# An add of tap products in a convolution and state-space kernel: by VectorE, or by an accumulating transfer inside SBUF issued by GpSimd

## The chip, the cores and the metric

The kernel runs on one core of a Trainium2 chip. The metric is the device time of one execution in microseconds (us), as the median of its runs; lower is better. A profile is one execution, recorded by the hardware profiler, with its own span. Engines are named as in the profile: PE (TensorE's matmuls; PEld its weight loads), DVE (VectorE), ACT (ScalarE), POOL (GpSimd) and SP (SyncE, which issues loads).

## The reference

Two independent layers over a sequence of S = 2048 with D = 1024 channels, all in bf16; their outputs stand side by side in the last dimension.

```
# A: gated convolution
k_shift[s] = sum over t of k[s - 3 + t] * shift_k[:, 3 - t]     # 4 taps, per channel
kv = k_shift * v
y  = irfft(rfft(kv, 2S) * rfft(ssm_k, 2S))[:S]  + kv * ssm_D    # long causal convolution
a  = q * y
# B: diagonal complex state space model
h[t] = Lam_bar * h[t-1] + x[t] @ B_bar^T
b = 2 * Re(h @ C^T) + x * Dskip
out = concat([a, b], -1)
```

The change is in the first line of A: the sum of the four tap products.

## The kernel before

**Tiling of A.** A row s of the sequence is written s = 16 n1 + n2, with n1 (128 values) on the partitions and n2 = 0 to 15 as the number of a tile. For each n2, four steps make one tile of kv, [128 x 1024] bf16:

- kvm(n2), lines 547 to 555: multiplies four neighbouring rows of k (from a ring of eight, `kring`) by the four taps (`wbc`): a tile `m` of [128 x 4 x 1024], some 2.3 us on DVE, in one instruction or, where the ring wraps, in two (L553, L555).
- kva(n2), line 560: adds the upper two products to the lower two, in place: `m[:, 0:2] += m[:, 2:4]`, 2048 elements on each partition. This is the changed line.
- kvb(n2), line 566: adds the last two into `st["kv", n2]` (named acc in the profile).
- kvc(n2), line 568: multiplies by v.

Then PE transforms the tile along n1 (am(n2, w), L573, four matmuls), ACT copies the results out of PSUM (ae, L580), and GpSimd stores them to HBM (ast, L582, tensor `Ys_kv`). The filter ssm_k takes the same way: hT and hc transpose it, hd adds ssm_D into one row (L605, on DVE), hm multiplies by the same matrix (L612), he copies out (L618), hst stores (two transfers each, L625, tensor `Ys_h`). When all 16 tiles of both are in HBM, the second stage loads them back in another layout (lk and lh, L635), transforms along n2 (sk, sh: L642), multiplies (pr, L667), transforms back (sa, L676), and a third stage (a3, L702) ends with q (qm, L712) and the output.

**Layer B** goes on beside it in 16 chunks of 128 rows: U (L462, matmuls with B), ue (ACT), r1 and r2 (rotation, DVE: L474, L483), rc, sc (scan, L493), cm, ca, r3, r4 (DVE), y (L517, matmuls with C), ye, yst. B's tile for the rotation products has the same name and slots as kvm's `m`.

**Order.** Nothing is scheduled by a tool: a hand-written list, ORDER (from line 66), names the tasks one after another, such as `kvm.4:m1 kva.4 kvb.4:b6`. Each engine takes its part of the list in order. `kva.4` is kva with n2 = 4; what follows the colon are the slots of the ring buffers that a task takes: `m0` and `m1` (two slots for products), `b0` to `b14` (2 KB per partition: kv, ysb, ysbh and others), `a..` (larger), `p0` to `p7` (PSUM banks). A task that takes a slot waits until the last user of the slot is done, the store of an output slot among them. The framework sets all semaphores from the tiles that an instruction reads and writes. The tap tasks run in the order n2 = 1, 3, 2, 0, 4, 6, 5, 7, 8, 10, 9, 13, 11, 12, 15, 14 (kvm), all in the first 180 us; kva in the order 3, 1, 2, 0, 4, 6, 5, 7, 10, 9, 8, 11, 12, 15, 14, 13. Some stretches of the list, with other tasks left out:

```
kvm.1:m0 ... kvm.3:m1 ... kva.3 stt ... kvb.3 ... kva.1 ... kvm.2:m1 ... kva.2 kvb.1 kvc.1 kvm.0:m0 kvb.2 kvc.2 kva.0 kvb.0 kvc.0 kvc.3
he.1.1.3 hst.1.1.1 ... kvm.4:m1 kva.4 kvb.4:b6 ... yst.1 ... hst.0.1.0 kvm.6:m0 kva.6 he.1.3.2:b3 ... kvm.5:m1 ... kvb.6:b8
hst.2.0.0 kva.5 ue.5.2 kvc.6 kvb.5:b7 kvc.5 ... kvm.7:m0 ... hst.2.3.1 hm.2.2.0:p4 kva.7 kvb.7:b1 kvc.7
kvm.10:m1 kva.10 kvb.10:b11 ... kvm.9:m1 kva.9 kva.8 kvb.8:b5 kvb.9:b6 ... kvm.11:m0 kva.11 ... kvb.11:b3
kvm.12:m0 ... kva.12 ... kvb.12:b4 kvc.12 kvm.15:m0 kva.15 kvb.15:b0 ... kvm.14:m0 ... kva.14 kva.13 kvb.14:b1 kvc.14
```

**Queues.** SP issues all loads. GpSimd issues nearly all stores (`gpd`), one after another and in the order of the list; it does next to nothing else. An issue that waits holds up those behind it.

Of the kernel before, what the change touches and what calls it, by code (L numbers as in the profile page):

```python
# [14 lines left out]
ALU = mybir.AluOpType  # L15
# [161 lines left out]
def full_kernel(ctx, tc, A_q, A_k, A_v, A_shift_k, A_ssm_k, A_ssm_D, B_x, B_Lre, B_Lim, B_Bre, B_Bim,  # L177
# [3 lines left out]
    nc = tc.nc  # L181
# [375 lines left out]

    def kva(n2):
        m = st["km", n2]
        nc.vector.tensor_add(m[:, 0:2, :], m[:, 0:2, :], m[:, 2:4, :])  # L560
    E["kva"] = kva

    def kvb(n2):
# [217 lines left out]
```

## Time and profile before

| | |
|---|---|
| median of 2 runs | 395.23 us (393.83 to 396.62) |
| span of the profiled execution | 399.6 us, 4.4 above that median |
| PE / DVE / ACT / POOL busy | 361.3 / 331.0 / 281.3 / 92.9 us |
| L560 (kva) on DVE | 16 instructions, 1205 to 1227 ns each, first at 25.8, last at 175.1 us |
| L566 (kvb) on DVE | 16 instructions, 671 to 693 ns each |
| DMA | 101.38 MB, mean 254 GB/s |
| chain that ended last | PE 43%, DMA 21%, issue 13%, ACT 9%, POOL 6%, DVE 5% |

In the timelines a row has its start and its length in us, the engine, the line, the operation, what is written and read, the count (rows that follow one another are merged, "x2"), and in brackets the idle time ahead of it with what ended it. The slices of the page cut the span into 40 equal parts of 10 us; a digit is the busy share in tenths. The issue rows give a transfer, the queue, the number, the size of one and the median us from issue to landing. The wait rows give who waited for whom: total us, times, longest. The DVE rows of L560 and L566 belong to kva and kvb in the order given above, so the n-th row of L560 is the n-th kva of the list; in the same way the rows of L582 and L625 on POOL are ast and hst.

### The profile page before, as it was taken

Reading aid. Unit: us, or ns where it says so; the run is one execution under the profiler, and the core shown is the slowest. Engines: PE = TensorE matmul, PEld = TensorE weight load, DVE = VectorE, ACT = ScalarE, POOL = GpSimd, SP = SyncE. Lnnn points to the kernel's source line nnn. Section 1 sums busy time; section 2 is a strip of 40 time slices with the busy share of each in tenths; the row PEclk is TensorE's granted clock in tenths of the full one; section 3 lists DMA queues with packets and bytes.
Section 4 is the critical chain, followed back from the end, with each engine's and each line's share of the span. In section 5 each row is a group of like instructions: output and inputs, shape, how many; then the busy total and the mean of one; then the engine's idle time right before and its main releaser. Section 6 shows DMA issues by size and latency. Waiting matters only on the chain.

```text
span 399.6 us, 8799 instructions
## 1 busy us (share of the span) xinstructions
PE 361.3 (90%) x3486; PEld 245.6 (61%) x3529; DVE 331.0 (83%) x335; ACT 281.3 (70%) x519; POOL 92.9 (23%) x156
## 2 busy tenths in 40 slices
PE   4899997998999887998999998999889999999990
PEld 2799986665665755886755644555335577744440
DVE  4999999997789588689989986989949558999920
ACT  4998888857688854778598787778657785374440
POOL 2000022465655763433001010110011003001450
PEclk9999999999999996999999999999999999999997
DMA  6999996578976898697898969979596987899781
GB/s 240 286 294 275 281 194 229 164 246 301 286 218 226 197 242 219 167 347 229 237 232 265 328 194 287 268 238 310 170 300 198 300 201 310 300 388 347 264 308 60
DMA packets 61124, 101.38 MB, mean 254 GB/s; under 512 B 31102, under 2 KB 33150, under 8 KB 61084
## 3 DMA queue, kind: packets, MB, share of 16 engines
q1 hardware_dynamic: 50428, 67.13, 60.3%
q0 software_dynamic: 10656, 33.71, 23.6%
q8 instruction: 27, 0.44, 0.5%
q14 instruction: 13, 0.11, 0.1%
HBM read 52.57 MB, written 33.55 MB: 216 GB/s over the span
## 4 chain that ended last, share of the span: by engine, by line
PE 43%; DMA 21%; issue 13%; ACT 9%; POOL 6%; DVE 5%; SPq 1%; another core or an unknown queue 1%; POOLq 0%; ACTq 0%; DVEq 0%
PE ps_u L462 16%; PE ps_y L517 11%; DMA Ys_h<-ysbh 8%; PE ps_a L676 5%; DMA hab<-hab 4%; PE ps_a L642 4%; DMA Ys_kv<-ysb 4%; POOL Ys_h L625 3%; ACT ysbh L618 2%; ACT hab L650 2%; POOL Ys_kv L582 2%; DMA l2k<-Ys_kv 1%; DMA wts<-a_c_W 1%; PE ps_t L427 1%; ACT vsb L683 1%
## 5 line engine op out<-in xcount | busy, mean ns | idle before, releaser
L462 PEld LDWEIGHTS <-BT 128*128 128x128 bf16 x2048 | 121.4, 99 | 12.0 <-issue 1.7
L517 PE MATMUL ps_y<-CT,h 128*128 128x512 bf16 x491 | 126.8, 381 | 2.1 <-ACT ysbh L618 1.2
L462 PE MATMUL ps_u<-xT,BT 128*128 128x128 bf16 x2048 | 127.5, 220 | 0.5 <-DVE BT L438 0.3
L517 PEld LDWEIGHTS <-h 128*128 128x128 bf16 x512 | 45.9, 98 | 43.8 <-issue 0.6
L493 DVE TENSOR_TENSOR_SCAN h<-rtab,h 128x1024 bf16<-128x1024 f32 x32 | 71.9, 2280 | 0.4
L667 DVE TENSOR_TENSOR hab<-x,hab 128x2048 bf16<-128x2048 bf16 x32 | 38.3, 1222 | 21.8 <-DMA hab<-hab 17.4
L625 POOL DMA_DIRECT2D Ys_h<-ysbh x64 | 46.0, 721 | 31.2 <-ACT ysbh L618 29.6
L464 ACT CAST u<-ps_u 128x512 bf16<-128x512 f32 x64 | 38.0, 613 | 13.0 <-PE ps_u L462 12.4
L618 ACT CAST ysbh<-ps_a 128x512 bf16<-128x512 f32 x64 | 35.5, 604 | 14.6 <-DMA Ys_h<-ysbh 5.6
L650 ACT CAST hab<-ps_a 128x512 bf16<-128x512 f32 x64 | 35.9, 620 | 12.3 <-PE ps_a L642 10.5
L656 ACT CAST x<-ps_a 128x512 bf16<-128x512 f32 x64 | 36.5, 614 | 10.6 <-PE ps_a L642 9.8
L580 ACT CAST ysb<-ps_a 128x512 bf16<-128x512 f32 x64 | 35.5, 614 | 11.0 <-DMA Ys_h<-ysbh 3.8
L683 ACT CAST vsb<-ps_a 128x512 bf16<-128x512 f32 x64 | 36.0, 618 | 5.6 <-PE ps_a L676 5.6
L474 DVE TENSOR_TENSOR mt<-u,Z 128x4096 bf16<-128x4096 bf16 x16 | 36.5, 2284 | 2.1 <-ACT u L464 2.1
L582 POOL DMA_DIRECT2D Ys_kv<-ysb x32 | 17.6, 553 | 87.1 <-ACT ysb L580 87.0
L685 POOL DMA_DIRECT2D Vs<-vsb x16 | 8.5, 534 | 124.5 <-ACT vsb L683 111.1
L474 DVE TENSOR_TENSOR mt<-h,Z 128x4096 bf16<-128x4096 bf16 x16 | 36.6, 2287 | 0.2
L676 PE MATMUL ps_a<-hab,wts 128*128 128x512 bf16 x125 | 32.6, 379 | 2.5 <-DVE hab L667 2.2
L528 ACT CAST yo<-ps_y 128x512 bf16<-128x512 f32 x32 | 19.0, 605 | 21.0 <-PE ps_y L517 16.6
L553 DVE TENSOR_TENSOR mt<-kring,wbc 128x4096 bf16<-128x4096 bf16 (+3 forms) x16 | 30.0, 1883 | 0.1
L612 PE MATMUL ps_a<-hT,F1t 128*128 128x256 bf16 x128 | 21.8, 276 | 7.8 <-ACT ysb L580 2.7
L522 PE MATMUL ps_y<-Dd,xT 128*128 128x128 bf16 x128 | 28.0, 219 | 0.3
(108 smaller groups left out, 417.4 us busy)
## 6 DMA issues: line engine op xcount, KB each, us to landing
Ys_kv<-ysb POOLq DMA_DIRECT2D x32, 256.0 KB, 3.5
Ys_h<-ysbh POOLq DMA_DIRECT2D x64, 128.0 KB, 3.7
l2h<-Ys_h SPq DMA_DIRECT2D x16, 512.0 KB, 5.2
hab<-hab SPq DMA_DIRECT2D x64, 128.0 KB, 5.6
l2k<-Ys_kv SPq DMA_DIRECT2D x16, 512.0 KB, 5.2
Vs<-vsb POOLq DMA_DIRECT2D x16, 512.0 KB, 5.8
vv<-Vs SPq DMA_DIRECT2D x32, 256.0 KB, 5.5
kring<-in_A_k_dram SPq DMA_DIRECT2D x8, 512.0 KB, 4.7
```

Of the source, the lines that this page charges most:

```text
L462: nc.tensor.matmul(pu[:, w, jl, :], BT[:, 2 * jp + jl, w, d, :], xT[:, d, :], start=(d == 0), stop=(d == ND - 1))
L464: E["ue"] = lambda i, jp: nc.scalar.copy(st["u", i][:, :, 2 * jp:2 * jp + 2, :], st["pu", i, jp][:])
L474: nc.vector.tensor_mul(m, s_, win(Z))
L493: nc.vector.tensor_tensor_scan(gf, rt1, gf, 0.0, ALU.mult, ALU.add)
L517: nc.tensor.matmul(py[:], h[:, 1 - w, j, :], CT[:, j, w, dh * 512:(dh + 1) * 512], start=(j == 0 and w == 0), stop=(j == NJ - 1 and w == 1))
L618: nc.scalar.copy(st["yh", qd, n4, w // 2][:, :, w % 2, :], st["pa", qd, n4, w][:].rearrange("p (c d) -> p c d", c=2))
L625: gpd(Ys_h[cc, n0:n0 + 2, :, qd * DQ:(qd + 1) * DQ].rearrange("n k d -> k n d"), t_[:, cc, :, :])
L650: nc.scalar.copy(st["hab", g][:, 0, cols], pt[:])
L656: nc.scalar.copy(st["x16", g][:, w * 512:(w + 1) * 512], st["ps", "l2k", g, w][:])
L667: nc.vector.tensor_mul(hab[:], st["x16", g][:].unsqueeze(1).to_broadcast([P, 2, D]), hab[:])
L676: nc.tensor.matmul(pt[:], st["w", gq][:, gi, 1 + a, :], hab[:, a, w * 512:(w + 1) * 512], start=(a == 0), stop=(a == 1))
L683: nc.scalar.copy(st["vsb", gq][:, gi, w * 512:(w + 1) * 512], st["ps", "v", g, w][:])
```

## The change

kva(n2) is no longer an instruction of DVE. GpSimd issues a transfer that reads `m[:, 2:4, :]` in SBUF and adds it to `m[:, 0:2, :]` in SBUF: 128 partitions of 2048 elements, 512 KB. ORDER is not changed, so the issue stands on GpSimd's queue where kva stands in the list. The framework lets the issue wait for kvm(n2) and lets kvb(n2) wait for the end of the transfer.

```diff
     def kva(n2):
         m = st["km", n2]
-        nc.vector.tensor_add(m[:, 0:2, :], m[:, 0:2, :], m[:, 2:4, :])
+        nc.gpsimd.dma_start(m[:, 0:2, :], m[:, 2:4, :], accum_op=ALU.add)
     E["kva"] = kva
```

## The prediction

> **What bounds the kernel now.** I read the page first (busy shares, slices), then VectorE's (DVE's) and GpSimd's (POOL's) timelines for the stretch in which the changed line runs (20 to 180 us), then the DMA issues and the waits.
>
> ```profile
> PE 361.3 (90%) x3486; PEld 245.6 (61%) x3529; DVE 331.0 (83%) x335; ACT 281.3 (70%) x519; POOL 92.9 (23%) x156
> ...
> DVE  4999999997789588689989986989949558999920
> ...
> PEclk9999999999999996999999999999999999999997
> ```
>
> No engine is free: PE is busy 90% of the span, DVE 83%. Until 90 us DVE is full; from 90 to 180 it has small gaps, while PE's slices stay at 8 or 9. Every engine issues in the order of the hand-written list, so a late result of one stops the next in line on another. GpSimd, at 23%, looks idle, but it issues the stores, in order.
>
> ```profile
> 88.92 1.23 DVE L560 TENSOR_TENSOR mt<-mt 128x2048 bf16<-128x2048 bf16 x1
> 92.79 0.69 DVE L566 TENSOR_TENSOR acc<-mt 128x1024 bf16<-128x1024 bf16 x1 [2.64 <-DMA Ys_h<-ysbh]
> ...
> 143.78 2.36 DVE L560 TENSOR_TENSOR mt<-mt 128x2048 bf16<-128x2048 bf16 x2
> 146.23 1.29 DVE L566 TENSOR_TENSOR acc<-mt 128x1024 bf16<-128x1024 bf16 x2
> ...
> 160.56 1.22 DVE L560 TENSOR_TENSOR mt<-mt 128x2048 bf16<-128x2048 bf16 x1
> 165.14 0.69 DVE L566 TENSOR_TENSOR acc<-mt 128x1024 bf16<-128x1024 bf16 x1 [3.36 <-DMA Ys_h<-ysbh]
> ...
> 168.79 1.23 DVE L560 TENSOR_TENSOR mt<-mt 128x2048 bf16<-128x2048 bf16 x1
> 170.21 0.69 DVE L566 TENSOR_TENSOR acc<-mt 128x1024 bf16<-128x1024 bf16 x1 [0.19 <-ACT ysb L580]
> ```
>
> In these DVE lines the second add (kvb, L566) stands close behind the first (kva, L560): 0 to 4 us lie between. Whatever replaces L560 has to be done within that.
>
> ```profile
> 94.73 1.43 POOL L625 DMA_DIRECT2D Ys_h<-ysbh  x2 [1.89 <-ACT ysbh L618]
> ...
> 105.39 1.43 POOL L625 DMA_DIRECT2D Ys_h<-ysbh  x2
> 114.38 4.32 POOL L625 DMA_DIRECT2D Ys_h<-ysbh  x6 [7.57 <-ACT ysbh L618]
> ...
> 181.29 0.54 POOL L582 DMA_DIRECT2D Ys_kv<-ysb  x1 [2.04 <-ACT ysb L580]
> ```
>
> GpSimd's timeline: most issues wait for an ACT eviction (the bracket). An issue put behind one of them inherits that wait.
>
> ```profile
> Ys_kv<-ysb POOLq DMA_DIRECT2D x32, 256.0 KB, 3.5
> Ys_h<-ysbh POOLq DMA_DIRECT2D x64, 128.0 KB, 3.7
> ...
> Vs<-vsb POOLq DMA_DIRECT2D x16, 512.0 KB, 5.8
> ```
>
> The last number is the time from issue to landing in us: 5.8 for 512 KB from GpSimd's queue.
>
> ```profile
> ACT ysbh L618 <- DMA Ys_h<-ysbh: 5.6, 4, 2.9
> ...
> PE ps_a L573 <- DVE acc L568: 0.7, 1, 0.7
> ```
>
> Two links already bind somewhere: ACT waits for stores to free its output slots, and PE waits for the finished kv tile (L568). Delays on DVE and GpSimd therefore have a way back into ACT and PE.
>
> **The change, part by part.**
>
> *Removed:* 16 adds on DVE at 1.22 us (L560), 19.6 us of DVE time, all before 177 us.
>
> *Added:* 16 issues on GpSimd at 0.54 to 0.74 us (its DMA rows), about 9 us on a queue 23% busy; and 16 transfers of 512 KB which read their destination too.
>
> *The new wait.* kvb(n) must wait until the transfer has landed. I call "lag" the time from the start of the issue to that moment. The trace has no accumulating transfer. Lower end 3.5 us (Ys_kv row, 256 KB); upper end 10.4: two rows of this queue, 256 KB in 3.5 and 512 KB in 5.8, differ by 2.3 per 256 KB, and if the extra read of 512 KB costs as much again, that is 5.8 + 4.6. I take 5.8, the row of the same size and queue: both ends of this transfer lie in SBUF, which should pay part of the extra read. The Trainium skill (DMA: Bandwidth & Descriptors, Anatomy of one DMA) gives about 2.0 us plus bytes at 436 GB/s, and its page Collectives: The Full Stack (Why ReduceScatter is half of AllGather) says an adding transfer reads two sources; my estimate from both is 2.0 + 1.05 MB/436 GB/s = 4.4 us, and the sum below would then be +45 and the time 440. The Vs row, 5.8 for a plain 512 KB where that formula gives 3.2, speaks for the longer lag.
>
> *The new order.* In the changed program's order on GpSimd, kva.4 stands behind hst.1.1.1 (the pair of Ys_h stores at 94.73), kva.6 ahead of hst.1.2.0 (101.17), kva.5 behind hst.2.0.0 (ends 118.7), kva.7 behind hst.2.3.1 (ends 133.0), kva.11 behind hst.3.3.0 (ends 162.6), kva.14 behind ast.15.1 (ends 181.8). So two things add up: the transfer starts only when GpSimd gets to it, and then takes the lag. I walk the sites with lag 5.8; "before" is the start in the trace.
>
> 1. kva.3, .1, .2, .0 (25.8 to 42.5 us): GpSimd is idle, and 16 short DVE instructions cover kva.3's lag. Four adds go (4.9 us) and the lags of kva.3, .2 and .0 come: kvb.0 at 44.0 instead of 42.5, +1.5; the 0.45 us gap at 71 us takes some back.
> 2. kva.4: product ready at 90, GpSimd there at 96.2 (94.73 + 1.43). kvb.4 at 102.0 instead of 92.8: **+9.2**.
> 3. kva.6: GpSimd is free at 100.6, but the product now ends at 109.9 (100.7 + 9.2), and the queue stands still until then. Behind it are hst.1.2.0, ast.3.0, hst.0.0.0, ast.3.1, hst.1.3.1; the last ends at 115.9 instead of 106.8. ACT's he.2.0.2 reuses the slot that this store empties (111.6 in the trace, 4.7 after the store's issue): 120.6, so ACT is +9.0. kvb.6 at 115.7, +7.7.
> 4. kva.5: hst.2.0.0 follows he.2.0.1 on ACT, now 127.8. kvb.5 at 133.6 instead of 114.3: **+19.3**. PE's am.5.3 needs kvc.5: 134.9 instead of 119.0, and PE stands for some 7 us. hm.3.0.2 needs hd.3, on DVE behind it: PE +17.6.
> 5. kva.7: behind hst.2.3.1, 133.0 + 17.1 = 150.1. kvb.7 at 155.9 instead of 128.8: **+27.1**. PE's am.7.3: +21.6.
> 6. kva.10: product at 161.7 (134.6 + 27.1), kvb.10 at 167.5, +26.8 (in the trace it waits 4.84 us for a store, which covers most of the lag).
> 7. kva.9, kva.8: kvm.9 reuses kva.10's slot, ends 3.0 later at 170.5; kva.8 is issued behind kva.9, 0.57 later, so 6.4 follow: kvb.8 at 176.9 instead of 146.2, **+30.7**. kvc.8 ends at 179.5, and am.8.0 waits for it: PE +30.6.
> 8. kva.11: behind hst.3.3.0, 162.6 + 30.6 = 193.2; kvb.11 at 199.0 instead of 156.4: **+42.6**.
> 9. kva.12, kva.15: same slot (m0) one after the other, each product 3.7 after the last kvb, then the lag: kvb.12 at 208.4 (+43.3), kvb.15 at 217.9 (**+47.7**); am.15.2: PE +47.2.
> 10. kva.14, kva.13: behind ast.15.1, 181.8 + 47.2 = 229.0; kvb.14 at 234.8 (**+58.6**), kvc.13 ends at 237.6 instead of 179.9: **+57.8**.
>
> The 19.6 us that DVE saves are inside this walk: each DVE stretch is copied without its L560. From here on the order is that of before, so I carry the 57.8 to the end. What hides nothing here: in the trace PE waits 1.27 us at 180.6 right behind this point.
>
> *The clock.* PE stood still from 150 to 152.9 in the trace, and the slice at 150 to 160 has a granted clock of 0.6; 32 matmuls of L462 then took 3.37 us instead of 1.95. The walk gives PE some six stalls of 4 to 10 us. Most of the slowed work lies beside DVE's new waits; I add 2 us, out of 0 to 5. The Trainium skill (TensorE: Matmul & The Clock Gate, Part 1: The HAM clock gate) puts the drop to half rate behind an idle window of about 3.4 us; by it nearly each of these stalls brings one, and the term would be its upper end, 5.
>
> **Sum.** 57.8 + 2 = +60. The profiled execution (399.6 us) would become 459; it lies 4.4 above the median of the runs, 395.2, and with the same distance the median becomes 455. Ten lags follow one another in the walk, so a microsecond of lag is worth about 10: lag 3.5 gives +37 (with the clock's 0 to 5, 432 to 437), lag 10.4 gives +102 (497 to 502).
>
> **The rivals.**
>
> - *Lag without echo.* ACT, PE and the stores keep their old times, and only DVE's own chain is late. For it: PE and ACT have gaps (ACT is 70% busy). Against: steps 3, 4 and 7 name instructions that need the late results. The walk with the old store times gives kvb.4 +9.2, kvb.5 +10.2, kvb.8 +14.6, kvb.15 +22.4, kvc.13 +25: 420 us.
> - *A slow transfer.* Lag 8 to 10.4 or more, because the destination's read is paid like other bytes, or issuing takes longer. For it: the 2.3 us per 256 KB between two rows. Against: both sides in SBUF, and lighter DMA traffic once the stage is stretched. 475 to 500.
> - *Hidden, no slower.* The delay of the kv tiles disappears behind PE's other matmuls (U and y), and DVE's 19.6 us come free: 387 to 399, since DVE has 5% of the chain that ended last. It decides if kvc.13's delay is under the slack between it and PE's next need. For it: PE is 90% busy with work that needs no kv tile. Against: PE's order is fixed, and am.8.0 and am.14.0 wait in the trace already, 0.70 and 1.27 us, so the slack is about nil; and even with a lag of 2.9, the shortest landing of the page (out_dram<-ot), GpSimd's order alone delays kvb.4 by 6.
> - *That the change does nothing* can be excluded: L560 is gone from DVE's order, and 16 issues of it are in GpSimd's.
>
> **How the numbers follow.** Forecast (lag 3.5 to 8, with echo: 432 to 477) 0.66; lag without echo 0.13; slow transfer 0.16; hidden 0.05. The predicted time is the forecast's, 455. The range 424 to 495 leaves out the hidden case, most of the case without echo and the end of the slow one: about 2 in 10. Under 2% (8 us) is about what a measurement here can't tell from no change. All cases but the hidden one are slower by more: slower 0.95, same 0.03, faster 0.02 (the hidden case split).
>
> **What would show it.** Step 1: kvb.0 within 2 us of 42.5. Steps 2 to 10: the starts of L566 as given; L566's waits go to a transfer mt<-mt, in sum some 50 us or more on DVE; the DMA list shows mt<-mt with 5 to 7 us to landing; GpSimd's L560 has one long wait on DVE near 100 to 110 us. The stage from 85 to 180 us takes about 150 instead of 95, and from the L2 loads on the order and the distances are those of before. Wrong would be the prediction if L566 starts near its old times, if mt<-mt lands in under 3 or over 8 us, or if the later stages take back what the first lost.

## The result and the profile after

| | before | after |
|---|---|---|
| median of 2 runs, us | 395.23 (393.83 to 396.62) | 483.83 (483.69 to 483.97) |
| ratio, 95% interval | | 1.2201 [1.2005, 1.2397] |
| span of the profiled execution, us | 399.6 | 481.9 |
| mean granted clock of PE | 0.985 | 0.911 |

The changed kernel is 88.6 us slower. The forecast was +60, and its range ended at 495. In the experiments below a median is of all executions of a kernel, a ratio with its 95% interval of those alone that ran undisturbed, since some executions are a per cent or two slower than the rest.

The page of the changed kernel, busy shares, slices (12 us each now), two groups (busy, mean ns | idle time ahead and its cause) and two issue rows (KB, median us to landing):

```profile
PE 380.8 (79%) x3529; PEld 255.3 (53%) x3529; DVE 312.5 (65%) x319; ACT 282.7 (59%) x519; POOL 107.8 (22%) x172
...
DVE  4963199980932742133321989998898584799971
...
PEclk9998599998978889587986899999999989999999
...
L566 DVE TENSOR_TENSOR acc<-mt 128x1024 bf16<-128x1024 bf16 x16 | 11.0, 691 | 116.0 <-DMA mt<-mt 80.1
...
L573 PE MATMUL ps_a<-acc,F1t 128*128 128x512 bf16 x64 | 25.1, 459 | 63.7 <-DVE acc L568 57.1
...
mt<-mt POOLq DMA_DIRECT2D x16, 512.0 KB, 7.0
Ys_kv<-ysb POOLq DMA_DIRECT2D x32, 256.0 KB, 4.7
```

VectorE got what the change promised: 18.5 us less work (331.0 to 312.5). It now idles 116 us ahead of its 16 second adds (15 before), 80.1 of them put down to the new transfers. Of its thirteen slices from the 10th to the 22nd (108 to 265 us), eleven read 0 to 4; the slices of the same tasks before, the 9th to the 18th, read 5 to 9. PE passes this on: 57 us of waits for the finished kv tile, where 0.7 stood before. The stores of Ys_kv take 4.7 us to landing instead of 3.5.

The windows of the two stages (window, its length, then busy us of PE, PEld, DVE, ACT and POOL, granted clock, DMA share, GB/s; the share is the summed time of the packets over that of 16 engines, and can pass 1); of before, the stage of the tap tasks and the rest:

```profile
85.00:180.00 95.00, 85.43 (x877) 62.64 (x887) 76.97 (x72) 66.81 (x125) 49.75 (x75) 0.96 0.81 247
180.00:399.60 219.60, 200.82 (x1606) 118.96 (x1630) 176.20 (x145) 145.91 (x284) 27.26 (x51) 0.99 0.84 261
```

and of after, between the same tasks:

```profile
85.00:266.00 181.00, 112.95 (x1022) 78.09 (x1020) 80.71 (x77) 82.50 (x151) 70.72 (x101) 0.83 0.73 188
266.00:482.00 216.00, 204.68 (x1628) 120.56 (x1628) 176.17 (x145) 143.99 (x280) 26.89 (x50) 0.98 0.82 258
```

All of the loss lies up to 266 us. (The tasks of the first stretch, up to 85 us, are 18 us late, so part of them falls into the third window.) The rest takes 216.0 instead of 219.6 us: kvc.13, the last of the tap tasks, is 86.0 us late, B's last eviction ye.14.1 is 87.1 late, and behind that the profiled execution of before took 9.3 us to its end, that of after 4.5.

Where the loss arises is seen in VectorE's timeline, first kvb.0 before, then rows of after:

```profile
42.50 0.69 DVE L566 TENSOR_TENSOR acc<-mt 128x1024 bf16<-128x1024 bf16 x1
```

```profile
41.32 2.29 DVE L553 TENSOR_TENSOR mt<-kring,wbc 128x4096 bf16<-128x4096 bf16 x1 [1.69 <-DMA kring<-in_A_k_dram]
55.99 0.69 DVE L566 TENSOR_TENSOR acc<-mt 128x1024 bf16<-128x1024 bf16 x1 [12.38 <-DMA mt<-mt]
...
61.01 0.69 DVE L566 TENSOR_TENSOR acc<-mt 128x1024 bf16<-128x1024 bf16 x1 [3.60 <-DMA mt<-mt]
...
119.77 0.69 DVE L566 TENSOR_TENSOR acc<-mt 128x1024 bf16<-128x1024 bf16 x1 [12.89 <-ACT ysbh L618]
...
202.46 1.29 DVE L566 TENSOR_TENSOR acc<-mt 128x1024 bf16<-128x1024 bf16 x2 [13.54 <-DMA mt<-mt]
...
262.06 0.69 DVE L566 TENSOR_TENSOR acc<-mt 128x1024 bf16<-128x1024 bf16 x1 [18.17 <-DMA mt<-mt]
```

The rows of L566 in after are kvb.2, kvb.0, kvb.4, kvb.8 with kvb.9, and kvb.14. While they wait VectorE does nothing: what stands behind kvb in its order waits too. The bracket of kvb.4 names an ACT eviction, but that one ended before 113 us; GpSimd's timeline shows what lay between:

```profile
112.89 1.43 POOL L625 DMA_DIRECT2D Ys_h<-ysbh  x2 [2.51 <-ACT ysbh L618]
114.32 0.96 POOL L560 DMA_DIRECT2D mt<-mt  x1
...
128.03 0.92 POOL L560 DMA_DIRECT2D mt<-mt  x1 [8.93 <-DVE cm L498]
...
143.80 4.34 POOL L625 DMA_DIRECT2D Ys_h<-ysbh  x6 [9.44 <-ACT ysbh L618]
148.13 0.96 POOL L560 DMA_DIRECT2D mt<-mt  x1
```

kva.4 stands behind a pair of stores that waited for ACT, is issued at 114.32 and lands 5.2 us later; kva.6 then waits 8.9 us for VectorE, with eight stores behind it; kva.5 waits behind six stores. This is the circle of the prediction's steps 2 to 4.

**The lags** (start of an issue to its landing, us, in the order of the 16 issues): 7.5, 11.1 | 18.4, 17.1 | 5.2, 4.8, 4.8, 4.8, 4.9 | 6.6, 12.5 | 5.1, 4.7, 7.3 | 10.1, 12.0. Where little else moves, a transfer takes about 4.8. The first four, kva.9 with kva.8, and kva.14 with kva.13 take up to four times that. Each of these groups has transposing loads of x beside it or close ahead; SP's timeline, where the two longest lags begin (37.5 and 43.9 us):

```profile
35.70 6.73 SPq L451 DMA_TRANSPOSE xT<-in_B_x_dram  x1
...
44.81 12.52 SPq L451 DMA_TRANSPOSE xT<-in_B_x_dram  x1
```

In before no such issue takes more than 4.3 us, so both sides slow each other (no run shows by what mechanism): from 37 to 56 us the DMA engines are busy at a share of 1.17 and move 172 GB/s. One transposing load is not enough for it: kva.10 and kva.11 are issued 1.8 us behind one each (SP's issues at 179.09 and 212.72) and land in 4.9 and 5.1. The packet records show that single packets stand, and not that all go slowly. A 4096 B packet of an adding transfer takes 0.33 to 0.34 us in quiet times (a plain one of that size 0.16 to 0.17). From 37.5 to 61 us, where kva.2 and kva.0 land, the median of their 256 packets is still 0.33, but eight take over 0.5 us, one of them 5.0. Of the 1891 packets of 256 B in the same stretch the median is 0.02, but 70 take over 0.5 us, one of them 5.0; in all of before the longest such packet took 2.3. How these add up to lags of 18 us was not taken apart.

**The stores behind a transfer.** The six stores of Ys_h right behind kva.6 (128.63 to 134.35 us) and the same six before (101.17 to 106.82 us), each from the answer for L625 in that window:

```profile
DMA to landing us min/median/max: 5.1/7.1/7.8
...
DMA to landing us min/median/max: 3.8/4.9/5.8
```

The slot that ACT's he.2.0.2 waits for is therefore free some 2 us later than the queue's own delay would have it. The four stores right behind kva.8 are worse off: 12.1 to 12.7 us instead of 2.6 to 7.0.

### The profile page after: what moved, and what is told of

Its sections match the earlier page's. It is cut to its first block, busy times and chain, and to the rows that moved or that the text cites. A ratio compares the mean times of both kernels' runs of the same rounds, so it can differ in the third digit from the quotient of the medians.

```text
span 481.9 us, 8857 instructions
## 1 busy us (share of the span) xinstructions
PE 380.8 (79%) x3529; PEld 255.3 (53%) x3529; DVE 312.5 (65%) x319; ACT 282.7 (59%) x519; POOL 107.8 (22%) x172
## 4 chain that ended last, share of the span: by engine, by line
PE 25%; issue 16%; DMA 8%; DVE 4%; ACT 2%; POOL 2%; SPq 1%; DVEq 0%; POOLq 0%; ACTq 0%
PE ps_y L517 9%; PE ps_a L676 5%; PE ps_u L462 5%; PE ps_a L642 4%; DMA l2k<-Ys_kv 3%; DMA hab<-hab 1%; DVE mt L553 1%; DMA wts<-a_c_W 1%; DMA Ys_kv<-ysb 1%; DMA mt<-mt 1%; PE ps_a L702 1%; POOL Ys_kv L582 1%; DMA out_dram<-ot 1%; DVE hab L667 1%; DVE mt L555 1%
## 5 line engine op out<-in xcount | busy, mean ns | idle before, releaser
L462 PEld LDWEIGHTS <-BT 128*128 128x128 bf16 x2048 | 126.6, 101 | 13.7 <-issue 4.7
L462 PE MATMUL ps_u<-xT,BT 128*128 128x128 bf16 x2048 | 132.8, 225 | 0.8 <-DVE BT L438 0.7
L517 PE MATMUL ps_y<-CT,h 128*128 128x512 bf16 x512 | 132.7, 386 | 0.0
L566 DVE TENSOR_TENSOR acc<-mt 128x1024 bf16<-128x1024 bf16 x16 | 11.0, 691 | 116.0 <-DMA mt<-mt 80.1
L573 PE MATMUL ps_a<-acc,F1t 128*128 128x512 bf16 x64 | 25.1, 459 | 63.7 <-DVE acc L568 57.1
L517 PEld LDWEIGHTS <-h 128*128 128x128 bf16 x512 | 46.6, 100 | 45.5 <-issue 3.2
L618 ACT CAST ysbh<-ps_a 128x512 bf16<-128x512 f32 x64 | 35.3, 601 | 38.5 <-DMA Ys_kv<-ysb 19.3
L625 POOL DMA_DIRECT2D Ys_h<-ysbh x64 | 48.5, 815 | 41.7 <-ACT ysbh L618 41.7
L667 DVE TENSOR_TENSOR hab<-x,hab 128x2048 bf16<-128x2048 bf16 x32 | 38.2, 1221 | 23.4 <-DMA hab<-hab 13.5
L464 ACT CAST u<-ps_u 128x512 bf16<-128x512 f32 x64 | 37.9, 608 | 17.5 <-PE ps_u L462 17.2
L650 ACT CAST hab<-ps_a 128x512 bf16<-128x512 f32 x64 | 35.9, 617 | 14.4 <-PE ps_a L642 12.0
L573 PEld LDWEIGHTS <-F1t 128*128 128x128 bf16 x64 | 6.2, 108 | 68.6 <-DVE acc L568 51.1
L582 POOL DMA_DIRECT2D Ys_kv<-ysb x32 | 20.3, 660 | 74.8 <-ACT ysb L580 74.7
L676 PE MATMUL ps_a<-hab,wts 128*128 128x512 bf16 x128 | 34.0, 387 | 2.4 <-DVE hab L667 2.3
L612 PE MATMUL ps_a<-hT,F1t 128*128 128x256 bf16 x128 | 23.4, 298 | 12.4 <-ACT ysb L580 7.1
```

The lines of the kernel that those rows point to most:

```text
L462: nc.tensor.matmul(pu[:, w, jl, :], BT[:, 2 * jp + jl, w, d, :], xT[:, d, :], start=(d == 0), stop=(d == ND - 1))
L464: E["ue"] = lambda i, jp: nc.scalar.copy(st["u", i][:, :, 2 * jp:2 * jp + 2, :], st["pu", i, jp][:])
L517: nc.tensor.matmul(py[:], h[:, 1 - w, j, :], CT[:, j, w, dh * 512:(dh + 1) * 512], start=(j == 0 and w == 0), stop=(j == NJ - 1 and w == 1))
L625: gpd(Ys_h[cc, n0:n0 + 2, :, qd * DQ:(qd + 1) * DQ].rearrange("n k d -> k n d"), t_[:, cc, :, :])
L650: nc.scalar.copy(st["hab", g][:, 0, cols], pt[:])
L667: nc.vector.tensor_mul(hab[:], st["x16", g][:].unsqueeze(1).to_broadcast([P, 2, D]), hab[:])
```

## The experiments

The first theory was that of the prediction, with its lag corrected: the wait for the lag and the place on GpSimd's in-order queue, echoed by ACT and PE. The rivals were that the transfers slow the other traffic, the stores above all, whether anybody waits for them or not; that the adding, not the moving, is dear; and for the long lags, that general traffic rather than the transposing loads makes them. Each kernel was compared with the kernel before on the same chip, whose medians were 397.86 us beside first4, last12, plain and early, 397.75 beside after_plainx, before_plainx, beside and pick, and 398.42 beside the others. "Late by" is the start of a task against the profile of before. The code cuts show edits against the changed kernel, in 5 and 6 against the kernel before.

### 1. The first four tiles alone, and the last twelve alone

```diff
+        if n2 < 4:
             nc.gpsimd.dma_start(m[:, 0:2, :], m[:, 2:4, :], accum_op=ALU.add)
+        else:
+            nc.vector.tensor_add(m[:, 0:2, :], m[:, 0:2, :], m[:, 2:4, :])
```

This is first4; last12 has `n2 >= 4` in the first line.

> Transfers only for n2 = 0 to 3; the other twelve adds stay on VectorE. Theory W (the cost is the wait of kvb for the transfer, in VectorE's order, and is carried on): in the changed kernel kvb.0 started 18.5 us late, and this delay goes to the end: 411 to 416. If the cost went by the number of transfers (4 of 16 times 88.6): 417. By the walk as it was forecast (lag 5.8 us each): 397. If the later stages take a delay back: 395 to 400.

> Transfers only for n2 = 4 to 15; the first four adds stay on VectorE. Theory W: the changed kernel without the 18.5 us of its first four, 463 to 468, with kvb.4 about 8 to 9 us late as in step 2 of the forecast. By the number of transfers (12 of 16): 462. If the delays overlap and are not added, so that the first four are hidden by the rest: 478 to 484.

first4: 411.98 us (410.65 to 416.13), ratio 1.0377 [1.0296, 1.0459]: +14.1. last12: 469.08 us, 1.177 [1.1661, 1.1878]: +71.2. Together 85.3, against 88.6 for the whole change, so the two parts add up. In first4 kvb.0 is late by 17.1 us and kvc.13 by 11.5, so some of the delay is taken back on the way. last12 is a microsecond above what was expected, and its kvb.4 is late by 11.2 instead of 8 to 9, because the issue itself comes 2.6 us later than the stores of before would have it. The prediction had put the first four at +1.5: this is the largest single piece that it missed.

### 2. Moving without adding

```diff
-        nc.gpsimd.dma_start(m[:, 0:2, :], m[:, 2:4, :], accum_op=ALU.add)
+        nc.gpsimd.dma_start(m[:, 0:2, :], m[:, 2:4, :])
```

> The transfer copies and does not add: the same bytes, queue, place and waits, with the addition left out (the sum lacks two products). In the changed kernel a 4096-byte packet of the adding transfer took 0.33 to 0.34 us, that of a plain one of 4096 bytes 0.16 to 0.17; with 8 packets per engine that is 1.3 us per lag, ten lags in a row: 465 to 472 if the adding alone lengthens the lag, and less, 445 to 465, if the long lags of 17 to 18 us are also due to it. If adding costs nothing and the wait is all: 481 to 486.

457.2 us, 1.1521 [1.1434, 1.1608]: +59.3. Where the adding transfer lands in 4.7 to 5.2 us, the plain one lands in 2.9 to 4.3; an issue holds GpSimd for 0.55 us instead of 0.93. The transfers beside heavy traffic still take 8.8 and 11.1 (kva.2, kva.0) and 9.8 and 10.5 (kva.14, kva.13). So the adding costs about 29 of the 88.6 us, the long lags included, as the band of 445 to 465 had it, and two thirds of the loss come with a transfer of these bytes that only copies.

### 3. Issuing each transfer as soon as its product is there

```diff
-... kvm.5:m1 hc.2.0:b7 hd.2 ... hst.2.0.0 kva.5 ...
+... kvm.5:m1 kva.5 hc.2.0:b7 hd.2 ... hst.2.0.0 ...
```

Every kva moved in this way in ORDER, right behind its kvm.

> The changed kernel with each kva moved in the list to right behind its kvm: GpSimd issues the transfer as soon as it can, not behind the stores that stand between. Theory W: kva.4, .5, .7, .11 and .14 no longer wait for stores (5 to 10 us each in the walk), and kva.5, .7, .8 and .13 get cover: some 35 to 45 us less, 435 to 455, with the lag still paid at kvb.2, .0, .4, .10, .11, .12, .15, .14. If GpSimd's place in the order is no cause: 480 to 486.

463.88 us, 1.1625 [1.1523, 1.1727]: only 20 us better than the change, and outside what was expected. Six of the kva (4, 6, 9, 10, 11, 15) stood right behind their kvm already, so nothing moved for them, though the expectation had counted kva.4 and kva.11 in: kvb.4 is late by 8.8 more than kvm.4, as in after (9.0). For those that did move the gain is there (kvb.7 late by 27.6, not 46.0), but then the other side of the in-order queue shows, in GpSimd's timeline of this kernel:

```profile
213.76 0.86 POOL L560 DMA_DIRECT2D mt<-mt  x1 [10.79 <-DVE mt L555]
...
234.76 0.86 POOL L560 DMA_DIRECT2D mt<-mt  x1 [10.70 <-DVE carry L500]
235.33 2.97 POOL L582 DMA_DIRECT2D Ys_kv<-ysb  x5
```

GpSimd stands 10.8 us at kva.12 and 10.7 us at kva.14, issued early but with products that aren't ready, and the stores behind them stand too, five of Ys_kv behind kva.14. From 60 us on it waits 45.8 us at L560 for VectorE, and 33.0 in after. kvb.8 is late by 34.0, but kvb.11 by 53.4. Neither place in this queue is free.

### 4. Without the transposing loads

```diff
-        nc.sync.dma_start_transpose(st["xT", i][:], x[i * T:(i + 1) * T, :])
+        spd(st["xT", i][:].rearrange("p a b -> p (a b)"), x[i * T:(i + 1) * T, :])
```

after_plainx and before_plainx have this edit; after_noT and before_noT load C (CT, L445) plainly too. The bytes are the same, the values land untransposed.

> The changed kernel with the 16 transposing loads of x replaced by plain loads of the same bytes (x is not transposed, so layer B computes on other numbers). Theory T: a transposing transfer in flight is what stretches some lags (18.4 and 17.1 us for kva.2 and kva.0, 12.5 for kva.8, 10 and 12 for kva.14 and .13, where the others have 4.7 to 7.5). Then these five fall to 5 to 8, and the distance to before_plainx is 58 to 68 instead of 88.6. If it is the general load of the DMA engines, the lags stay above 10 and the distance is 80 to 90.

> The kernel before with the same replacement of x's transposing loads by plain ones: the base for after_plainx. Both theories: 390 to 397, since the loads of x are early enough.

after_plainx 471.47 us, 1.1803 [1.17, 1.1905]; before_plainx 398.0, 1.0011 [0.9973, 1.0049]: the distance is 73.5, between the two expectations. The lags of kva.2, kva.14 and kva.13 fell to 7.2, 6.0 and 7.9, kva.8's only from 12.5 to 11.0, and kva.0's is 19.0: CT's transposing loads moved up beside it (issues of 5.2 us at 44.25 and of 14.1 us for two at 49.48). Hence the second pair:

> The changed kernel with all transposing loads (16 of x, 8 of C) replaced by plain loads of the same bytes; x and half of C are not transposed, so layer B computes on other numbers. In after_plainx the lag of kva.2 fell from 18.4 to 7.2 us, but kva.0's was 19.0, now beside the transposing loads of C. Theory T: kva.2 and kva.0 land within 8 us, kvb.0 is at most 8 us late instead of 18.5 to 21.3, and the distance to before_noT is 62 to 72. If the small packets of 256 bytes do it (the plain loads of C have runs of 256 bytes too), or the load in general: kva.0 keeps 12 to 19 us and the distance is 74 to 88.

> The kernel before with the same replacement, the base for after_noT: 392 to 399 by every theory.

after_noT 466.24 us, 1.1709 [1.1635, 1.1783]; before_noT 398.53, 1.0009 [0.9966, 1.0053]: the distance is 67.7, as the theory of the transposing loads had it. The lags of kva.2 and kva.0, from the answers for L560 between 36 and 46 us, of after

```profile
DMA to landing us min/median/max: 17.1/17.7/18.4
```

and of after_noT:

```profile
DMA to landing us min/median/max: 5.9/7.4/9.0
```

The transposing loads make these two lags, and some 21 us of the 88.6 by the medians (12 by the profiled spans, 82.3 against 467.1 - 397.0). The general load doesn't explain it: from 40 to 60 us the DMA engines of after_noT have a share of 1.07, as in before, and move 254 GB/s, where after moved 155. But the transposing loads aren't the only cause: 9.0 and a late kvb.0 (10.8) are a little over what was expected, kva.1's lag is 12.9 here beside heavy plain loads, and kva.9 with kva.8 still take 7.8 and 10.9.

### 5. Adding transfers beside the old add, and nobody waits

```diff
         nc.vector.tensor_add(m[:, 0:2, :], m[:, 0:2, :], m[:, 2:4, :])
+        sp = tc.dram_tile([P, W], F32, name="sp%d" % n2)
+        nc.gpsimd.dma_start(sp[:, :], rt1, accum_op=ALU.add)
```

> The kernel before, with an adding transfer of 512 KB at each kva in addition, from a table in SBUF to a scratch tensor in HBM of its own, for which nothing waits: GpSimd's time and the traffic without the wait. Theory W: 395 to 402. Theory C (the traffic and GpSimd's time are what costs): 420 or more.

435.0 us, 1.0955 [1.0869, 1.1042]. The first theory had expected next to nothing and was wrong here: 16 adding transfers on GpSimd's queue cost 37 us although nothing waits for their results. The waits of this kernel show how; the last row is from SP's timeline:

```profile
ACT ysbh L620 <- DMA Ys_kv<-ysb: 13.7, 2, 11.8
...
POOL Ys_h L627 <- DMA Ys_h<-ysbh: 6.6, 2, 6.2
...
19.71 14.10 SPq L451 DMA_TRANSPOSE xT<-in_B_x_dram  x2
```

In before ACT's row (there L618) reads 2.2, 2, 1.4, and GpSimd waits for no store at all. The stores behind the transfers land later (Ys_kv 5.9 us instead of 3.5), so ACT's output slots come free later, and GpSimd's own issues wait for earlier transfers. Some 6.6 of the 37 us have another cause: these transfers wait for no product, so the first four go out together from 14.4 us on, beside two transposing loads whose issues take 14.1 us (4.2 in before). A load of k comes late behind them, and kvb.0 is late by 6.6 before any store is issued. A caution: these transfers are of 4-byte numbers, add into HBM, go out at other times and land in 8.8 us, not 7.0, so the 37 us aren't a share of the 88.6.

### 6. Only transfers that the walk holds to be free

kva.8 and kva.13 had the longest time between kvm and kvb. In pick these two are transfers, issued right behind their kvm; in pick13 kva.13 alone; all others are VectorE's adds.

```diff
-... kvm.13:m1 hst.3.2.0 ... ast.15.1 kva.14 kva.13 kvb.14:b1 ...
+... kvm.13:m1 kva.13 hst.3.2.0 ... ast.15.1 kva.14 kvb.14:b1 ...
```

> Only kva.8 and kva.13 by transfer, and moved in the list to right behind kvm.8 and kvm.13, which leaves 11 and 23 us until their kvb in the trace of before. Theory W: the lag is covered, VectorE has 2.4 us less to do: 392 to 395.5. If a transfer costs by itself (5.5 us each): 405.

> Only kva.13 by transfer, issued right behind kvm.13, some 23 us ahead of its kvb. Theory W: covered, VectorE has 1.2 us less to do: 395 to 398, the same as before. Theory C (a transfer costs by holding up the stores behind it, as pick's ACT waits suggest): 399 to 402.

pick: 405.0 us, 1.0134 [1.0057, 1.0212], pick13: 402.92, 1.0068 [1.0022, 1.0115]. pick came out as the expectation that a transfer costs by itself had it, pick13 just above its theory C. Even a transfer with time to spare gains nothing. In pick am.8.0 is late by 5.8, of which 1.9 were there already; between 130 and 165 us the waits show

```profile
ACT hT L603 <- DMA Ys_h<-ysbh: 4.7, 1, 4.7
```

where before has 1.4 (there L600): ACT waits for a store behind kva.8, and PE for ACT. But at am.9.3 PE is late by only 0.9 again, and by 3.9 from am.12.0 on, so this wait alone isn't shown to be the loss. pick13 doesn't settle it: its trace is late by 2.1 already at 31 us, long before its only transfer, and shows no loss where that stands (lag 5.0).

### 7. The add computed by GpSimd

```diff
-        nc.gpsimd.dma_start(m[:, 0:2, :], m[:, 2:4, :], accum_op=ALU.add)
+        nc.gpsimd.tensor_add(m[:, 0:2, :], m[:, 0:2, :], m[:, 2:4, :])
```

The same place on the same queue and the same wait of kvb, with no transfer.

> kva as an add computed by GpSimd itself: the same place in GpSimd's order and the same wait of kvb, but no transfer. No row of these traces has such an add; its length will be read from the run. Theory W alone: the shift follows the walk of the prediction with that length g as the lag (about +27 for 2.5 us, +45 for 4.4, +58 for 5.8), so 425 to 455 if g is 2.5 to 6. If it is the transfers among the stores that cost (theory C), the shift stays well under the walk: 400 to 415.

467.65 us, 1.1757 [1.1684, 1.1829]: +69.2, more than expected. Its page and, below, VectorE's timeline:

```profile
L560 POOL TENSOR_TENSOR mt<-mt 128x2048 bf16<-128x2048 bf16 x16 | 65.8, 4121 | 46.7 <-DVE mt L553 38.4
```

```profile
41.06 0.69 DVE L566 TENSOR_TENSOR acc<-mt 128x1024 bf16<-128x1024 bf16 x1
41.78 4.43 DVE L568 TENSOR_TENSOR acc<-acc,v 128x1024 bf16<-128x1024 bf16 x1
```

The add takes 4.1 us, for which the walk gives about +42 (nine lags, each 1.7 shorter than its 5.8); kvc.13 is late by 68.8, and by 58.3 if the 10.5 that kvm.4 is late are left out. Two things stand against the walk here: the queue is held 4.1 us per add instead of 0.9, and a VectorE instruction beside such an add is stretched (4.43 us for a multiply that takes 0.69). What each is worth was not measured. So a delay in this place costs much without any transfer, but how much of the 69 us is the delay alone, and what the contention of transfers adds in the changed kernel, can't be read off this run.

None of the twelve kernels is faster than the kernel before.

## Why the prediction was right, and where its sizes were off

How late the tasks are, in us. "From kvm.4" is the measured value less the 18.0 that kvm.4 itself is late, since the walk starts step 2 with no delay. "Measured lags" is the predicted value with the lag that each transfer took in the place of 5.8:

| step | task | predicted | measured lags | measured | from kvm.4 |
|---|---|---|---|---|---|
| 1 | kvb.0 | 1.5 | | 18.5 | |
| 2 | kvb.4 | 9.2 | 8.6 | 27.0 | 9.0 |
| 4 | kvb.5 | 19.3 | 17.7 | 38.7 | 20.7 |
| 5 | kvb.7 | 27.1 | 24.5 | 46.0 | 28.0 |
| 6 | kvb.10 | 26.8 | 23.3 | 45.2 | 27.2 |
| 7 | kvb.8 | 30.7 | 33.9 | 56.2 | 38.2 |
| 8 | kvb.11 | 42.6 | 45.1 | 63.5 | 45.5 |
| 9 | kvb.15 | 47.7 | 50.6 | 69.9 | 51.9 |
| 10 | kvb.14 | 58.6 | 65.8 | 85.8 | 67.8 |
| 10 | kvc.13 | 57.8 | 65.0 | 86.0 | 68.0 |

- **The mechanism held.** The direction, the stage, the echo into ACT (he.2.0.2 late by 11.4 from kvm.4, 9.0 foretold) and PE (am.5.3 17.5, am.7.3 22.5, against 15.9 and 21.6) and the long wait of kva.6 on VectorE came as written. The rival without echo and the hidden one fell with the same rows.
- **The time is in the range, but not where the forecast had it.** 484 us is above the forecast's own 432 to 477 and in the band of the rival "slow transfer" (475 to 500). Two of the prediction's own signs spoke against it: kvb.0 started 18.5 us late, not within 2, and six of the 16 transfers took over 8 us, though the median is 7.0.
- **That steps 4 to 6 came out within 1.4 us is partly luck.** The lag taken was 1 us too long at each place, and stood in for some 3 us that the walk lacks: with the measured lags it gives kvb.5 17.7 and kvb.7 24.5, where 20.7 and 28.0 were measured.
- **Step 1 was mis-sized, and is 18 of the 28 us that the walk lacked.** It gave the first four the lag of all others, 5.8; kva.2 and kva.0 had 18.4 and 17.1. The prediction looked at GpSimd's queue being idle there and not at what the DMA engines carried. From 40 to 60 us of before their share is 1.07, against 0.81 in the stage from 85 to 180 us, from which the rest of the walk comes; but the share alone isn't the cause, since after_noT has 1.07 too and lags of 5.9 and 9.0. Experiment 1 shows the size, and experiment 4 that the transposing loads are a good part of the cause.
- **The lag of 5.8 was too long for a quiet time (4.7 to 5.2) and too short for the busy ones.** The rival "slow transfer" (8 to 10.4) was thus right at some places and wrong as a general case. For the quiet time the estimate by the Trainium skill (DMA: Bandwidth & Descriptors, Anatomy of one DMA), 4.4, was closer than the row taken; the sum by it would have been further off, since the long lags carry it.
- **Steps 7 and 10 were mis-sized by the same thing.** kva.8's lag is 12.5 and kva.14's 10.1, each in a pair of transfers and beside transposing loads (SP's issues at 189.52 and 250.00). With C and x loaded plainly they are 10.9 and 7.5, so the load is part of it; what part the pair and the other traffic have was not taken apart.
- **With the measured lags the walk nearly closes.** Nine lags in a row (kva.4, .5, .7, .10, .8, .11, .12, .15, .14; the prediction spoke of ten) then give 65.0 at kvc.13, with the 18.0 of step 1 83.0, and 86.0 were measured. The 3.0 left over appear at kvb.5, and behind it the walk lacks a term: stores that land later behind an adding transfer. he.2.0.2 is late by 11.4 where 9.0 were foretold, and the stores that it waits behind took up to 7.8 us instead of 5.8. The gap is 4.3 at kvb.8 and 0.4 at kvb.11, so it isn't one fixed term; its share in the 88.6 is open.
- **The clock.** It went from 0.985 to 0.911 in the mean, 0.83 in the long stage, and PE's busy time from 361.3 to 380.8; but 43 more of its matmuls are in the record, which at 0.2 to 0.4 us each may be half of that. The prediction put most of the slowed work beside VectorE's waits. Whether the term was 2 us, or nearer its upper end of 5, was not tried by itself.

## What to carry to other kernels

An operation that moves to another queue is priced by three things, not by its length: where it stands in that in-order queue, how long it takes until its result is there, and who waits for it in order behind. Here 19.6 us of VectorE work in short adds were exchanged for 16 transfers of 5 to 18 us in a loop that passes every delay on, and 18 us of that came from a place where the issuing queue was idle but the DMA engines were not. Look at what loads run in each window, and of what kind (the DMA share alone did not tell it), before taking a transfer's landing time from another stage, and don't put transfers into the queue that carries the stores unless these have time to spare.

## What the runs showed of the hardware

- An adding transfer inside SBUF of 512 KB lands in 4.7 to 5.2 us in quiet times, a plain one at the same places in 2.9 to 4.3; the adding issue holds GpSimd for 0.93 us instead of 0.55, and each 4096 B packet takes twice as long (0.33 against 0.16 us).
- Adding transfers and transposing loads slow each other: lags of 17 to 18 us, a transposing issue of 12.5 us where 4.3 was the longest, and from 40 to 60 us 155 GB/s at a DMA share of 1.23, where before moved 235 GB/s at 1.07. Most packets keep their time and single ones stand for up to 5.0 us. Small packets aren't the whole reason, since none of 256 B in the plain loads of C took over 0.06 us; why two of the transposing loads did no harm is open.
- Stores of 128 KB right behind an adding transfer landed in 5.1 to 7.8 us (kva.6), where the same stores took 3.8 to 5.8 without one, and in 12.2 to 12.5 behind kva.8, where they took 7.0.
- A GpSimd add of 128x2048 takes 4.1 us, VectorE's 1.22, and a VectorE instruction beside it was stretched from 0.69 to 4.43 us, about the length of that add. The Trainium skill (SBUF — State Buffer, Who interferes with whom) says that a VectorE instruction with two inputs in SBUF contends with a GpSimd instruction that reads SBUF; the trace agrees.
